# A windowed-attention and feed-forward kernel: separate PSUM tiles, another order at the start, and earlier loads in the loop

## The chip, the cores and the metric

The kernel runs on one core of a Trainium2 chip. The core has a matrix engine (TensorE, "PE"; its weight loads are shown apart as "PEld"), a vector engine (VectorE, "DVE"), a scalar engine (ScalarE, "ACT"), GpSimd ("POOL") and SyncE ("SP"), each with its own queue of instructions that it works through in order. Data comes from and goes to device memory by 16 DMA engines, which POOL and SP feed here. PE writes its products to PSUM, from which ACT and DVE copy or compute into SBUF. The metric is the device time of one launch in microseconds; lower is better.

## The reference

There are 4 batches, 8 heads, 768 positions and head size 64. A query may see the keys of the last 96 positions and the first 8 keys of its batch; a bias falls with the distance, with one slope for each head. The attention output, 3072 tokens of 512, goes through a feed-forward layer of width 2048.

```python
scores = scale * np.matmul(q, k.transpose(0, 1, 3, 2))
is_global = pos[None, :] < int(n_global)                  # n_global = 8
is_local = (rel >= 0) & (rel < int(n_local))              # n_local = 96
dist = np.where(is_global & ~is_local, float(n_local), np.abs(rel))
scores = scores - slopes[:, None, None] * dist            # 8 slopes
scores = np.where(is_global | is_local, scores, -1e9)
a = softmax(scores)                                       # written out in the reference
x = np.matmul(a, v)                                       # -> (3072, 512)
h = x @ w_in                                              # (512, 2048)
r = np.maximum(h, 0.0)
out = (s * (r * r) + b) @ w_out                           # (2048, 512)
```

Inputs and the output are float32; the kernel multiplies in bf16.

## The kernel before

The 3072 tokens are cut into 12 granules of 256, three to a batch; `j` is the granule's number. The order of the instructions is written out by hand: each engine works through its own in the order in which the functions below are called.

**The steps for a granule.** `load_pairs` or `load_rows` (lines 86 and 96) and `load_v` (107) bring k, q and v from device memory through POOL's DMA queue, which also turns float32 into bf16. A granule's v comes in two pieces. k and q must be transposed: for granules 0 to 2 PE does it into PSUM (`T_mm`, 251) and ACT or DVE copies the result out (`T_ev`, 266); from granule 3 on DMA transposes do it, issued on SP (`XB`, 280). `KO` and `VO` (303, 318) collect on DVE the keys and values of the neighbouring block and the global ones. `S_mm` (353) makes the scores of a pair of heads, `hp` 0 to 3, and `S_post` (373) takes the exponential on ACT. For granules 0 and 1 the bias and the mask are added on PE before that, by products with a diagonal matrix (`SB_mm`, 343); later DVE multiplies the exponentials by a template made once per head (`make_tmpl`, 242). The result is the tile `pt`. `A` (392) multiplies `pt` with v on PE, and DVE divides by the row's sum and writes `xn`. `xn` is transposed to `xT` by PE (`XT_half`, 442; `XT_pe`, 427) or by DMA (`XT_dma`, 460). `P1` (476) multiplies by two of the 16 column blocks of w_in, ACT takes the relu, and DVE squares (`flush`, 471). `P2` (522 and 562) multiplies by w_out, and DVE scales and adds the bias row (`P2_out`, 534).

**PSUM tiles.** Tags name them: `scA` and `scB` for scores (two banks each), `av` for value products, `psh` (two buffers), `pso`. One tile of tag psh holds the transposed k and the transposed q of a half of a granule; `T_mm` makes it for the first of the two and finds it in `tps` for the second. In `P2_end` (596), for the last 128 tokens, the two column pieces (0 to 320 and 320 to 512) lie in the two halves of one scB tile.

**The start.** SP issues four loads of the first granule's q and k (lines 148 and 149), in float32 and by halves (heads 0 to 3, and 4 to 7), as "raw" pieces; `cast` makes them bf16 on DVE or ACT. POOL builds the identity and the mask base, and issues in this order: v of granule 0 (two pieces), k and q of granule 1, piece 0 of w_in, v of granule 1, pieces 1 to 7 of w_in, k, q and v of granule 2, and three of four pieces of w_out (188 to 199). `more_loads` (201), called later, adds granule 3, the last piece of w_out, and granule 4. Lines 606 to 731 are the written order of the start. `idle` (224) puts products of constants on PE that nobody reads.

**The loop.** `period(j, items, at)` (746) runs for granules 3 to 11. It makes the scores of granule `j` and its value products, with feed-forward pieces of the granules before it (`items`) between them. After `A(j, 0)` it calls `pace(j)` and `load_granule(j + 2)`. `pace` (123) copies one element of `xn[j]` on POOL, so POOL issues the six loads of granule j + 2 only after that `xn` has been written.

Of the kernel before, what the change touches and what calls it, by code (L numbers as in the profile page):

```python
# [18 lines left out]
def kernel(  # L19
# [76 lines left out]
    def load_rows(j, nm):  # L96
        b, g = bg(j)
        src = q if nm == "q" else k
        t = ldp.tile([P, GB, H, D], BF16, name=f"{nm}nat", tag=f"{nm}nat")
        nat[nm, j] = t  # L100
        for i in range(GB):
            sb = g * GB + i
            nc.gpsimd.dma_start(  # L103
                t[:, i, :, :], src[b, :, sb * P : (sb + 1) * P, :].rearrange("h p d -> p h d")
            )

    def load_v(j):
        b, g = bg(j)
        for i in range(GB):
            sb = g * GB + i  # L110
            nc.gpsimd.dma_start(  # L111
                vaug[b][:, sb, :, 0:D],
                v[b, :, sb * P : (sb + 1) * P, :].rearrange("h p d -> p h d"),
            )
# [6 lines left out]
    pdum = const.tile([1, 1], BF16, name="pdum")  # L121

    def pace(j):
        nc.gpsimd.tensor_copy(pdum[:], xn[j][0:1, 0, 0, 0:1])  # L124

    def load_w_in(i, n):
        w = DF // n
        nc.gpsimd.dma_start(  # L128
            w_in_bf[:, :, i * w : (i + 1) * w], w_in_view[:, :, i * w : (i + 1) * w]
        )  # L130

    def load_w_out(i, n=4):
        w = FC // n
        nc.gpsimd.dma_start(
            w_out_bf[:, i * w : (i + 1) * w, :], w_out_view[:, i * w : (i + 1) * w, :]
        )
# [14 lines left out]
    def cast(nm, half, eng=None):  # L151
        hs = slice(4 * half, 4 * half + 4)
        i, o = raw32[:, "kq".index(nm), hs, :], nat[nm, 0][:, hs, :]
        if eng is None:
            nc.vector.tensor_copy(o, i)
        else:
            nc.scalar.copy(o, i)
# [27 lines left out]
        base=NL - 1,  # L185
        channel_multiplier=1,
    )
    load_v(0)
    load_pairs(1, "k")
    load_pairs(1, "q")  # L190
    load_w_in(0, 8)
    load_v(1)
    for i in range(1, 8):
        load_w_in(i, 8)
    load_pairs(2, "k")
    load_pairs(2, "q")
# [2 lines left out]
        load_w_out(i)  # L199

    def more_loads():
        load_rows(3, "k")
        load_w_out(3)
        load_rows(3, "q")
        load_v(3)
        load_granule(4)
# [17 lines left out]
    def idle(n, tag="pso", cols=4 * P):  # L224
        ps = PS[tag].tile([P, 4 * P], F32, name="ps_i", tag=tag)
        for _ in range(n):
            nc.tensor.matmul(
                ps[:, 0:cols],
                lhsT=nc.const_aps.tensor(1.0, (P, P), BF16),
                rhs=nc.const_aps.tensor(1.0, (P, cols), BF16),  # L230
                start=True,
                stop=True,
            )
# [8 lines left out]
    def make_tmpl(h):  # L242
        slope = float(2.0 ** (-8.0 * (h + 1) / H))
        nc.scalar.activation(
            tmpl[:, h, :], base[:].rearrange("p a c -> p (a c)"), ACT.Exp, scale=slope
        )
# [1 line left out]

    tps = {}

    def T_mm(j, half, nm, tag="psh"):
        a = 0 if nm == "k" else 1
        if (j, half) not in tps:
            tps[j, half] = PS[tag].tile([P, 2, 2, GT], BF16, name="ps_t", tag=tag)
        ps = tps[j, half]
        for e in range(2):
            hp = 2 * half + e
            for i in range(GB):
                for hi in range(2):
                    nc.tensor.transpose(  # L260
                        ps[hi * D : (hi + 1) * D, a, e, i * P : (i + 1) * P],
                        nat[nm, j][:, 2 * hp + hi, i * D : (i + 1) * D],
                        ident[:],
                    )

    def T_ev(j, half, nm, eng=None):
        b, g = bg(j)
        a = 0 if nm == "k" else 1
        if j not in qT:
            qT[j] = qtp.tile([P, HP, GT], BF16, name="qT", tag="qT")  # L270
        src = tps[j, half][:, a, :, :].rearrange("p e (i t) -> p e t i", i=GB)
        hs = slice(2 * half, 2 * half + 2)
        dst = kT[b][:, hs, g * GT : (g + 1) * GT] if nm == "k" else qT[j][:, hs, :]
        dst = dst.rearrange("p e (t i) -> p e t i", i=GB)
        if eng is None:
            nc.vector.tensor_copy(dst, src)
        else:
            nc.scalar.copy(dst, src)  # L278
# [64 lines left out]
    def SB_mm(j, hp, which=None):  # L343
        ps = sc_tile(j, hp, which)
        n = ncols(j)
        c0 = 0 if n == 3 * P else P
        m = base[:].rearrange("p a c -> p (a c)")[:, c0 : c0 + n]
        for hi in range(2):
            nc.tensor.matmul(  # L349
                ps[:, hi, 0:n], lhsT=diag[:, 2 * hp + hi, :], rhs=m, start=True, stop=False  # L350
            )
# [21 lines left out]
    def S_post(j, hp, biased=False):  # L373
        n = ncols(j)
        ps = sps.pop((j, hp))
        pt = ppool.tile([P, 2, 4 * P], BF16, name="pt", tag="pt")
        pts[j, hp] = pt
        nc.scalar.activation(pt[:, :, 0:n], ps[:, :, 0:n], ACT.Exp, scale=QSCALE)  # L378
        if not biased:
            c0 = 0 if n == 3 * P else P  # L380
            m = tmpl[:, 2 * hp : 2 * hp + 2, c0 : c0 + n]
            nc.vector.tensor_tensor(pt[:, :, 0:n], pt[:, :, 0:n], m, ALU.mult)  # L382
# [190 lines left out]
    def P2_cols(j, tb, ps, lo, hi):  # L573
        b, g = bg(j)
        flush()
        for fc in range(FC):
            nc.tensor.matmul(  # L577
                ps[:, 0 : hi - lo],
                lhsT=gT[j][:, fc, tb * P : (tb + 1) * P],
                rhs=w_out_bf[:, fc, lo:hi],  # L580
                start=(fc == 0),
                stop=(fc == FC - 1),
            )
        o_sb = work.tile([P, hi - lo], F32, name="o_sb", tag="o_sb", bufs=5)
        nc.vector.scalar_tensor_tensor(
            out=o_sb[:],
            in0=ps[:, 0 : hi - lo],
            scalar=s_bc[:],
            in1=bvec[:, lo:hi],
            op0=ALU.mult,  # L590
            op1=ALU.add,
        )
        t0 = b * S + g * GT + tb * P
        nc.sync.dma_start(out[t0 : t0 + P, lo:hi], o_sb[:])

    def P2_end(j, tb):
        ps = ps_b.tile([P, 2, DM], F32, name="ps_2e", tag="scB")
        P2_cols(j, tb, ps[:, 0, :], 0, 320)
        P2_cols(j, tb, ps[:, 1, :], 320, DM)

    def P2_sc(j, tb, which):
        pool, tag = ((ps_a, "scA"), (ps_b, "scB"))[which]
        po[j, tb] = pool.tile([P, 2, DM], F32, name="ps_2s", tag=tag)[:, 0, :]


    idle(7)
    SB_mm(0, 0)
    SB_mm(0, 1)
    cast("k", 0)
    T_mm(0, 0, "k")  # L610
    T_ev(0, 0, "k")
    cast("q", 0, "act")
    idle(2)
    T_mm(0, 0, "q")
    T_ev(0, 0, "q", "act")
    cast("k", 1)
    idle(1)
    T_mm(0, 1, "k")
    T_ev(0, 1, "k")
    cast("q", 1)  # L620
    idle(1)
    for hp in range(2):
        S_mm(0, hp, True)
        S_post(0, hp, True)
    T_mm(0, 1, "q")
    T_ev(0, 1, "q")
    more_loads()
    SB_mm(0, 2)
    S_mm(0, 2, True)
    S_post(0, 2, True)  # L630
    SB_mm(0, 3)
    S_mm(0, 3, True)
    S_post(0, 3, True)
    A(0, 0)
    A(0, 1, "pso")
    A(0, 2)
    A(0, 3, "pso")
    XT_half(0, 0, "act", "av")
    T_mm(1, 0, "k")
    T_mm(1, 1, "k")  # L640
    XT_half(0, 1, "dve", "pso")
    T_ev(1, 1, "k", "act")
    T_ev(1, 0, "k")
    SB_mm(1, 0)
    SB_mm(1, 1)
    T_mm(1, 0, "q")
    T_ev(1, 0, "q", "act")
    T_mm(1, 1, "q")
    T_ev(1, 1, "q", "act")
    KO(1)  # L650
    S_mm(1, 0, True)
    S_post(1, 0, True)
    S_mm(1, 1, True)
    S_post(1, 1, True)
    P1(0, 0)
    SB_mm(1, 2)
    S_mm(1, 2, True)
    S_post(1, 2, True)
    VO(1)
    A(1, 0)  # L660
    SB_mm(1, 3)
    S_mm(1, 3, True)
    S_post(1, 3, True)
    P1(0, 1)
    A(1, 1, "pso")
    make_tmpl(0)
    make_tmpl(1)
    A(1, 2)
    P1(0, 2)
    A(1, 3, "pso")  # L670
    P1(0, 3)
    XT_half(1, 0, "act", "av")
# [60 lines left out]
    def run(items, n):  # L733
        for _ in range(n):
            if items:
                f, *a = items.pop(0)
                f(*a)
# [7 lines left out]

    def period(j, items, at, late=None):
        SS(j, (0, 1))
        run(items, at[0])
        A(j, 0)
        if j + 2 < NJ:  # L750
            pace(j)
            load_granule(j + 2)
        run(items, at[1])
        A(j, 1)
        SS(j, (2, 3))
        if j + 1 < NJ:
            KO(j + 1)
        run(items, at[2])
        A(j, 2)
        run(items, at[3])  # L760
        A(j, 3)
        if late is None:
            XT_dma(j)
        if j + 1 < NJ:
            VO(j + 1)
        if j + 2 < NJ:
            XB(j + 2)
        if late is not None:
            run(items, 1)
            late()  # L770
            XT_pe(j, "act", "psh")
        run(items, 100)
# [80 lines left out]
```

## Time and profile before

| | |
|---|---|
| Median of 14 runs | 224.15 us (221.87 to 227.75) |
| The profiled execution | 227.26 us, of which its span is 225.5 us |
| PE busy | 211.3 us, 94% of the span |
| PEld busy | 143.4 us |
| DVE busy | 137.2 us |
| ACT busy | 115.4 us |
| POOL busy | 68.7 us |
| Mean rate of the DMA engines | 122 GB/s |
| Software queue (POOL's loads) | 13.11 MB in 72896 packets |
| Hardware queue (SP's transfers) | 14.17 MB in 34288 packets |

The span runs from the first instruction of the profiled execution to its last; its time, 227.26 us, has 1.76 us more around it. The profile's times are microseconds from the start of the span. Among its views are: busy tenths of each engine in 40 slices; groups of instructions by line with the mean duration; the chain of waits, which goes back from the last instruction to whatever released each step; windows, which give for any stretch the busy time of each engine, the TensorE clock that was granted (1.00 is full speed), the share of DMA time and the rate; and DMA issues with the time from issue to landing. A group's name reads out<-in, by the program's tile names. "Idle before" with an arrow names what an engine waited for.

### The profile page before, as it was taken

What the parts mean: (1) busy time and instruction counts of PE and PEld (TensorE: products, weight loads), DVE (VectorE), ACT (ScalarE), POOL (GpSimd) and SP (SyncE); (2) the same over time, 40 slices, a digit from 0 to 9 for tenths busy, and PEclk for the clock granted to TensorE, in tenths of its full rate; (3) what the DMA queues carried; (4) which work ended last, traced back from release to release, by engine and by line L of the source; (5) the groups of instructions that cost most, each with busy time, mean ns of one, the idle gap of its engine ahead of it and who ended that gap; (6) DMA issues with size and microseconds to landing.
All of it is one profiled execution on the core that took longest, in us unless ns stands there. A gap on an engine that the chain in (4) does not pass through costs nothing.

```text
span 225.5 us, 4962 instructions
## 1 busy us (share of the span) xinstructions
PE 211.3 (94%) x1997; PEld 143.4 (64%) x2029; DVE 137.2 (61%) x321; ACT 115.4 (51%) x176; POOL 68.7 (30%) x92
## 2 busy tenths in 40 slices
PE   8858999999999999999996999999999999999992
PEld 3435887645765775676763676675776676765762
DVE  3535557679988686656763484674684675752431
ACT  6525988842765645644443454645545645541420
POOL 8646664440072540620810360450530000000000
PEclk9967999999999999999998899999999999999998
DMA  5999999999969997997998299499796422031101
GB/s 156 101 177 195 189 189 195 179 148 120 86 42 150 209 156 125 145 175 95 158 171 113 62 117 165 102 153 128 113 168 114 71 77 66 0 95 47 47 27 69
DMA packets 107207, 27.60 MB, mean 122 GB/s; under 512 B 95792, under 2 KB 104240, under 8 KB 107184
## 3 DMA queue, kind: packets, MB, share of 16 engines
q0 software_dynamic: 72896, 13.11, 74.4%
q1 hardware_dynamic: 34288, 14.17, 33.3%
q8 instruction: 16, 0.26, 0.5%
q14 instruction: 7, 0.06, 0.1%
HBM read 27.26 MB, written 6.29 MB: 149 GB/s over the span
## 4 chain that ended last, share of the span: by engine, by line
PE 82%; DMA 7%; DVE 3%; issue 2%; ACT 2%; POOL 1%; SPq 1%; POOLq 0%; DVEq 0%; ACTq 0%
PE ps L483 36%; PE ps L526 29%; PE ps_av L410 5%; PE ps_s L365 5%; DMA vaug<-in_v_dram 4%; PE ps_2s L526 3%; DMA xT<-xn 3%; PE ps_2e L577 2%; DVE xn L419 1%; PE ps_t L260 1%; ACT pt L378 1%; PE ps_s L349 1%; PE ps_x L449 1%; SPq L463 1%; ACT gT L492 0%
## 5 line engine op out<-in xcount | busy, mean ns | idle before, releaser
L483 PE MATMUL ps<-xT,w_in_bf 128*128 128x256 bf16 x768 | 95.4, 274 | 2.3 <-DMA xT<-xn 2.2
L492 ACT ACTIVATE gT<-ps 128x512 bf16<-128x512 f32 x96 | 57.3, 599 | 62.2 <-PE ps L483 61.3
L483 PEld LDWEIGHTS <-w_in_bf 128*128 128x128 bf16 x768 | 73.6, 98 | 20.7 <-issue 3.1
L526 PE MATMUL ps<-w_out_bf,gT 128*128 128x512 bf16 x308 | 79.4, 382 | 1.9 <-issue 0.8
L474 DVE TENSOR_TENSOR gT<-gT 128x512 bf16<-128x512 bf16 x96 | 40.2, 424 | 24.9 <-ACT gT L492 24.7
L526 PEld LDWEIGHTS <-gT 128*128 128x128 bf16 x368 | 33.8, 98 | 30.7 <-issue 0.6
L378 ACT ACTIVATE pt<-ps_s 128x1024 bf16<-128x1024 f32 (+1 forms) x48 | 43.1, 952 | 18.8 <-PE ps_s L365 18.8
L382 DVE TENSOR_TENSOR pt<-pt,tmpl 128x1024 bf16<-128x1024 bf16 (+1 forms) x40 | 26.1, 652 | 13.0 <-ACT pt L378 11.9
L124 POOL COPY pdum<-xn 1x1 bf16<-1x1 bf16 x7 | 1.7, 249 | 76.4 <-DVE xn L419 76.4
L111 POOL DMA_DIRECT2D vaug<-in_v_dram x24 | 21.6, 915 | 3.9 <-DMA w_out_bf<-in_moe_w_out_dram 3.0
L410 PEld LDWEIGHTS <-pt 128*128 128x128 bf16 x352 | 16.4, 99 | 9.4 <-DVE xn L419 3.0
L418 DVE RECIPROCAL rc<-ps_av 128x4 f32<-128x4 f32 x48 | 8.6, 180 | 21.5 <-PE ps_av L410 20.8
L419 DVE TENSOR_TENSOR xn<-ps_av,rc 128x256 bf16<-128x256 f32 x48 | 20.4, 424 | 2.1
L537 DVE SCALAR_TENSOR_TENSOR o_sb<-ps,s_bc,bvec 128x512 f32<-128x512 f32 x18 | 13.5, 748 | 12.6 <-PE ps L526 12.6
L410 PE MATMUL ps_av<-vaug,pt 128*128 128x65 bf16 x224 | 18.1, 198 | 3.1 <-DMA vaug<-in_v_dram 2.0
L103 POOL DMA_DIRECT2D knat<-in_k_dram x18 | 15.8, 883 | 5.6 <-PE ps L483 3.3
L103 POOL DMA_DIRECT2D qnat<-in_q_dram x18 | 15.9, 899 | 2.1 <-DMA w_out_bf<-in_moe_w_out_dram 1.7
L365 PE MATMUL ps_s<-qT,kT 64*128 64x128 bf16 x224 | 12.5, 218 | 1.0 <-ACT qT L278 0.5
L410 PE MATMUL ps_av<-vo,pt 128*128 128x65 bf16 x128 | 12.0, 193 | 0.0
L365 PEld LDWEIGHTS <-kT 64*128 64x128 bf16 x224 | 7.1, 94 | 6.9 <-issue 5.9
L365 PE MATMUL ps_s<-qT,ko 64*128 64x128 bf16 x128 | 8.0, 216 | 0.0
L128 POOL DMA_DIRECT2D w_in_bf<-in_moe_w_in_dram x8 | 6.0, 752 | 5.6 <-DMA vaug<-in_v_dram 3.4
(66 smaller groups left out, 112.5 us busy)
## 6 DMA issues: line engine op xcount, KB each, us to landing
out_dram<-o_sb SPq DMA_DIRECT2D x23, 256.0 KB, 2.6
vaug<-in_v_dram POOLq DMA_DIRECT2D x24, 128.0 KB, 6.2
knat<-in_k_dram POOLq DMA_DIRECT2D x18, 128.0 KB, 4.6
qnat<-in_q_dram POOLq DMA_DIRECT2D x18, 128.0 KB, 4.7
w_in_bf<-in_moe_w_in_dram POOLq DMA_DIRECT2D x8, 256.0 KB, 9.6
w_out_bf<-in_moe_w_out_dram POOLq DMA_DIRECT2D x4, 512.0 KB, 12.7
raw<-in_k_dram SPq DMA_DIRECT2D x2, 256.0 KB, 4.1
raw<-in_q_dram SPq DMA_DIRECT2D x2, 256.0 KB, 4.3
```

Source lines behind the costliest of these rows:

```text
L103: nc.gpsimd.dma_start(t[:, i, :, :], src[b, :, sb * P : (sb + 1) * P, :].rearrange("h p d -> p h d"))
L111: nc.gpsimd.dma_start(vaug[b][:, sb, :, 0:D], v[b, :, sb * P : (sb + 1) * P, :].rearrange("h p d -> p h d"),)
L365: nc.tensor.matmul(ps[:, hi, oc * P : (oc + 1) * P], lhsT=kt[r, :], rhs=qT[j][r, hp, i * P : (i + 1) * P], start=not biased, stop=not bias ...
L378: nc.scalar.activation(pt[:, :, 0:n], ps[:, :, 0:n], ACT.Exp, scale=QSCALE)
L382: nc.vector.tensor_tensor(pt[:, :, 0:n], pt[:, :, 0:n], m, ALU.mult)
L410: nc.tensor.matmul(av[:, i, hi, :], lhsT=pt[:, hi, c * P : (c + 1) * P], rhs=vv, start=n_ == 0, stop=n_ == len(ops) - 1,)
L419: nc.vector.tensor_tensor(xn[j][:, :, 2 * hp : 2 * hp + 2, :], av[:, :, :, 0:D], rc[:].to_broadcast((P, GB, 2, D)), ALU.mult,)
L474: nc.vector.tensor_tensor(gs, gs, gs, ALU.mult)
L483: nc.tensor.matmul(ps[:, i, :], lhsT=w_in_bf[:, kc, fc * P : (fc + 1) * P], rhs=xT[j][:, kc, :], start=(kc == 0), stop=(kc == KC - 1),)
L492: nc.scalar.activation(gs, ps[:], ACT.Relu)
L526: nc.tensor.matmul(po[j, tb], lhsT=gT[j][:, fc, tb * P : (tb + 1) * P], rhs=w_out_bf[:, fc, :], start=(fc == 0), stop=(fc == FC - 1),)
L537: nc.vector.scalar_tensor_tensor(out=o_sb[:], in0=po[j, tb], scalar=s_bc[:], in1=bvec[:], op0=ALU.mult, op1=ALU.add,)
```

## The change

The function `T_mm` gets a flag `own`, with which it makes a tile of its own instead of sharing that of the other operand, and `T_ev` can copy out one of its two head pairs alone. The start uses these for the first granule's q: its first half goes to a tile of tag pso, its second to one of tag av, and the last copy is made in two parts. In the order of the start, the first k transposes come ahead of the first two `SB_mm`; `A(0,0)` comes ahead of the fourth pair's scores; the transposes of granule 1's k come between value products; its q transposes and their copies are interleaved with `XT_half`; `P1(0,0)` comes before granule 1's first scores, and `P1(0,1)` and `P1(0,2)` one step sooner; the filler products are two fewer and use tag av.

On POOL a one-element copy of the first raw k piece is put ahead of `load_v(0)`, so the loads wait for that piece. Piece 1 of w_in goes ahead of granule 1's v, and the last piece of w_out ahead of granule 3's k. In the loop, `pace` reads `pts[j, 0]` (the first pair's masked exponentials) instead of `xn[j]`, and it and `load_granule` are called right after the first two pairs' scores. `P2_end` takes an scA tile for the first column piece and an scB tile for the second.

```diff
     def pace(j):
-        nc.gpsimd.tensor_copy(pdum[:], xn[j][0:1, 0, 0, 0:1])
+        nc.gpsimd.tensor_copy(pdum[:], pts[j, 0][0:1, 0, 0:1])
...
+    nc.gpsimd.tensor_copy(pdum[:], raw32[0:1, 0, 0, 0:1])
     load_v(0)
     load_pairs(1, "k")
     load_pairs(1, "q")
     load_w_in(0, 8)
+    load_w_in(1, 8)
     load_v(1)
-    for i in range(1, 8):
+    for i in range(2, 8):
         load_w_in(i, 8)
...
     def more_loads():
+        load_w_out(3)
         load_rows(3, "k")
-        load_w_out(3)
         load_rows(3, "q")
...
-    def T_mm(j, half, nm, tag="psh"):
+    def T_mm(j, half, nm, tag="psh", own=False):
         a = 0 if nm == "k" else 1
-        if (j, half) not in tps:
+        if own or (j, half) not in tps:
             tps[j, half] = PS[tag].tile([P, 2, 2, GT], BF16, name="ps_t", tag=tag)
         ps = tps[j, half]
+        tps[j, half, nm] = ps
...
-    def T_ev(j, half, nm, eng=None):
+    def T_ev(j, half, nm, eng=None, es=(0, 1)):
...
-        src = tps[j, half][:, a, :, :].rearrange("p e (i t) -> p e t i", i=GB)
-        hs = slice(2 * half, 2 * half + 2)
+        e0, e1 = es[0], es[-1] + 1
+        src = tps[j, half, nm][:, a, e0:e1, :].rearrange("p e (i t) -> p e t i", i=GB)
+        hs = slice(2 * half + e0, 2 * half + e1)
...
     def P2_end(j, tb):
-        ps = ps_b.tile([P, 2, DM], F32, name="ps_2e", tag="scB")
-        P2_cols(j, tb, ps[:, 0, :], 0, 320)
-        P2_cols(j, tb, ps[:, 1, :], 320, DM)
+        for pool, tag, lo, hi in ((ps_a, "scA", 0, 320), (ps_b, "scB", 320, DM)):
+            ps = pool.tile([P, 2, DM], F32, name="ps_2e", tag=tag)
+            P2_cols(j, tb, ps[:, 0, :], lo, hi)
...
-    idle(7)
-    SB_mm(0, 0)
-    SB_mm(0, 1)
+    idle(7, "av")
     cast("k", 0)
     T_mm(0, 0, "k")
     T_ev(0, 0, "k")
+    SB_mm(0, 0)
+    SB_mm(0, 1)
     cast("q", 0, "act")
-    idle(2)
-    T_mm(0, 0, "q")
+    T_mm(0, 0, "q", "pso", True)
     T_ev(0, 0, "q", "act")
     cast("k", 1)
-    idle(1)
+    idle(1, "av")
     T_mm(0, 1, "k")
     T_ev(0, 1, "k")
     cast("q", 1)
-    idle(1)
     for hp in range(2):
         S_mm(0, hp, True)
         S_post(0, hp, True)
-    T_mm(0, 1, "q")
-    T_ev(0, 1, "q")
+    idle(1, "av")
+    T_mm(0, 1, "q", "av", True)
+    T_ev(0, 1, "q", None, (0,))
+    T_ev(0, 1, "q", None, (1,))
     more_loads()
     SB_mm(0, 2)
     S_mm(0, 2, True)
     S_post(0, 2, True)
+    A(0, 0, "pso")
     SB_mm(0, 3)
     S_mm(0, 3, True)
     S_post(0, 3, True)
-    A(0, 0)
-    A(0, 1, "pso")
-    A(0, 2)
-    A(0, 3, "pso")
-    XT_half(0, 0, "act", "av")
+    A(0, 1)
+    A(0, 2, "pso")
     T_mm(1, 0, "k")
     T_mm(1, 1, "k")
-    XT_half(0, 1, "dve", "pso")
+    T_ev(1, 0, "k", "act")
+    A(0, 3)
+    XT_half(0, 0, "act", "pso")
+    SB_mm(1, 0)
+    T_mm(1, 0, "q")
+    XT_half(0, 1, "dve", "av")
     T_ev(1, 1, "k", "act")
-    T_ev(1, 0, "k")
-    SB_mm(1, 0)
+    T_ev(1, 0, "q")
     SB_mm(1, 1)
-    T_mm(1, 0, "q")
-    T_ev(1, 0, "q", "act")
     T_mm(1, 1, "q")
     T_ev(1, 1, "q", "act")
     KO(1)
+    P1(0, 0)
     S_mm(1, 0, True)
     S_post(1, 0, True)
     S_mm(1, 1, True)
     S_post(1, 1, True)
-    P1(0, 0)
+    P1(0, 1)
...
     VO(1)
-    A(1, 0)
     SB_mm(1, 3)
     S_mm(1, 3, True)
     S_post(1, 3, True)
-    P1(0, 1)
+    A(1, 0)
     A(1, 1, "pso")
+    P1(0, 2)
     make_tmpl(0)
     make_tmpl(1)
     A(1, 2)
-    P1(0, 2)
...
     def period(j, items, at, late=None):
         SS(j, (0, 1))
-        run(items, at[0])
-        A(j, 0)
         if j + 2 < NJ:
             pace(j)
             load_granule(j + 2)
+        run(items, at[0])
+        A(j, 0)
```

## The prediction

> **What bounds the kernel now.** I read the slices first: where PE is full, and at which clock.
>
> ```profile
> PE   8858999999999999999996999999999999999992
> PEclk9967999999999999999998899999999999999998
> ```
>
> A slice is 5.64 us. From the sixth on PE is nearly always busy, so time is to be had only in the first four slices, around slice 22, and at the very end. The groups agree: PE is busy 211.3 of 225.5 us, and the next engine, DVE, 137.2. I then read the chain of waits over the start, and the windows over the stretch it points to.
>
> ```profile
> 2.55 0.95 POOL vaug L111
> 3.50 9.89 DMA vaug<-in_v_dram
> ...
> 13.43 0.39 PE ps_av L410 x4
> ```
>
> Start, length, what: the chain stands on the second piece of v for 9.89 us. Nothing after it can be attention until 13.43.
>
> ```profile
> 9.35:12.77 3.42, 1.66 (x20) 0.84 (x19) 0.69 (x1) 2.10 (x3) 0.07 (x1) 0.99 1.74 153
> 12.77:16.18 3.41, 2.09 (x28) 1.57 (x25) 2.07 (x8) 0.00 (x0) 2.23 (x3) 0.50 1.91 177
> 16.18:19.60 3.42, 3.20 (x26) 1.71 (x25) 1.62 (x4) 1.17 (x2) 2.22 (x4) 0.51 1.57 194
> ```
>
> Stretch, its length, then busy us of PE, PEld, DVE, ACT, POOL; granted clock, DMA share, GB/s. PE was half busy in the first stretch, and the clock fell to 0.50 near 12.7. It stayed there through a stretch that was 61% busy, and came back near 19.5, after one that was 94% busy. So the wait for v costs twice: idle PE, then slow PE.
>
> The same windows by the microsecond show what v waited for:
>
> ```profile
> 5.00:6.00 1.00, 1.00 (x11) 0.53 (x10) 0.19 (x1) 0.28 (x1) 1.00 (x2) 1.00 0.96 209
> ...
> 8.00:9.00 1.00, 0.57 (x15) 0.37 (x16) 0.91 (x2) 0.59 (x1) 1.00 (x2) 1.00 0.26 14
> 9.00:10.00 1.00, 0.81 (x10) 0.42 (x11) 0.58 (x1) 0.92 (x2) 0.42 (x1) 1.00 1.48 96
> ```
>
> Up to about 7 the DMA engines carry mainly the raw q and k pieces from SP's queue. By queue, GpSimd's moved 115 packets from 5 to 6, 281, 409, 111, and then some 700 in each us from 9 on. v's two pieces were issued at 2.49 and 3.44.
>
> **The profiled run against the median.** Its span is 225.5, its time 227.26 (1.76 outside the span), the median 224.15. Here the 3.1 us lie:
>
> ```profile
> 119.20:139.40 20.20, 17.86 (x160) 11.78 (x164) 10.75 (x26) 8.63 (x12) 5.54 (x7) 0.92 1.08 117
> 139.40:155.60 16.20, 16.04 (x160) 11.26 (x164) 9.55 (x22) 8.53 (x12) 5.50 (x7) 1.00 1.14 132
> ```
>
> One period of the loop took 20.2 us where the next took 16.2: the chain shows xT<-xn issued at 114.9 and landing only at 121.9, and the clock at 0.50 behind it. Without these 4.0 us the run is at 223.3, so I take the median run as one mostly without this stall, and take all gains from 224.15.
>
> **Part by part.**
>
> *The end.* Of the last token block, the second column piece waits until DVE has read the first, in the other half of the same PSUM tile:
>
> ```profile
> 217.85 2.19 PE ps_2e L577 x16
> ...
> 220.06 0.56 DVE o_sb L585
> ...
> 220.66 1.49 PE ps_2e L577 x16
> ```
>
> With two tiles the second piece starts at 220.04, not 220.66: **0.6 us**, with nothing beside it; ps_a's tile was read last by DVE at 209.30 + 0.75, so no new wait. Late next is PE itself.
>
> *k and q in separate PSUM tiles, transposes ahead of the mask products.* T_mm(0,0,"q") no longer waits for the k copy (0.19 us), k's transposes no longer stand behind four mask products (knat ready 4.64, PE there at 5.13), and the last q copy (0.69) is cut in two so that S_mm(0,2) starts after half. Together some 1 us, but all of it before v lands: **nothing**, hidden by v's wait. Two fewer filler products (0.22 to 0.4 each) are hidden by the same wait. If v came before about 10 they would count.
>
> *The copy ahead of load_v(0).* POOL now waits for the first raw k piece (DVE's cast of it started at 3.81), copies one element, and issues v. In the loop such a copy starts 0.54 us before the next load's issue, so v is issued near 4.4 instead of 2.49: **1.9 us later**, and behind it all of POOL's queue: k and q of granule 1, w_in, v of granule 1. What this does to v's landing the trace does not show; both ends:
>  - Late end: v keeps its 10.0 us from issue to landing. The second piece lands at 15.3.
>  - Early end: v is as quick as a v load in the loop (5.8 us, two at a time). Its second piece, issued near 5.3, lands at 11.1.
>  - Between: the raw pieces, alone, are through near 6.3 (0.93 MB were moved by 6, at up to 324 GB/s); GpSimd's queue starts 2.5 us after the issue, as before, near 7; v's 2048 packets (2 x 128 KB in rows of 64 bf16) at 700 per us take 2.9; landings then lagged the bytes by about 3 (0.262 MB were through near 10.1, the second piece landed at 13.4). This gives **12.9**, and I take it: it is worked from the queue's own packets.
>
>  A rule speaks against this edit. The Trainium skill, "DMA: Bandwidth & Descriptors", section "Issuing engines are not separate DMA queues", says that transfers run on the same 16 engines and interleave whichever engine issued them, so holding v back creates no bandwidth. Pure interleaving would make it late by up to 1.9. The rows show the engines not filled while v waits (14 GB/s from 8 to 9), which that rule does not explain; so I stay at 0.5 sooner.
>
> *Value products between the scores.* A(0,0) now stands in PE's queue before SB_mm(0,3) and S_mm(0,3). While v is out, these 8 matmuls wait behind it, and ACT's fourth exp with them: PE idles longer before v (about 9.9 to 12.9), so I expect the clock to fall again. After v the work fills the gaps in which A waited for DVE. I sum PE's queue from v to the end of P1(0,0), S_mm(1,0) and S_mm(1,1), in the cold durations of the trace: four A at 0.5; SB_mm(0,3) 2 x 0.32 (as the cold 384-column ones at 3.7) and S_mm(0,3) about 0.5 (estimate from 0.34 warm); 16 k transposes 1.0; XT halves 0.61 + 0.54; SB_mm(1,0) and (1,1) 4 x 0.43; 16 q transposes 1.0. Sum 8.0 cold, to which the warm P1(0,0), 0.98, and 16 score products, 0.62, are added. Before, all this ended at 22.30.
>
>  When does the clock return? In the trace, after a stretch 94% busy. The new queue is dense from 12.9, so one stretch earlier: near 16.2, with 3.2 of the 8.0 done and 4.8 left, which at full clock is about 2.5 (16 q transposes fell from 1.0 to 0.47). I add 0.3 for copies that ACT and DVE owe: 19.0; with 1.6 more 20.6: a gain of **1.7**. If it returns only at 19.5: 6.6 done, 1.4 left is 0.7, so 20.2 + 1.6 = 21.8: a gain of 0.5. Here too a rule stands against it: the Trainium skill, "TensorE: Matmul & The Clock Gate", Part 4, says that transposes don't count as busy for the clock. By it the dense stretch, with some 0.8 us of transposes, is only 70% busy, and the answer is 0.5. The row: the stretch from 16.18 had only 1.4 us of other products, yet it brought the clock back. I take 1.7.
>
> *P1(0,0) sooner* is in that sum: it fills the 0.46 us in which PE waited for ACT's qT copy at 20.24. w_in 0 landed at 17.6 and w_in 1 (now ahead of v(1)) near 20.6, in time. v(1) comes one w_in later, 1.4 us, from 19.4 to 20.8; VO(1) needs it at 19.85, before A(1,0) at 23.06: DVE may stand 1 us, with slack behind.
>
> *Loads in the loop.* pace(j) waits for the first masked pt instead of A(j,0)'s xn. In the period from 103.3 pt was ready at 105.2, xn's copy started at 107.60: six loads (5.3 us of issue) start 2.4 us sooner. Late next: nothing on PE, since k and q are transposed at the period's end. Their tail leaves xT<-xn freer, and collides with the q transposes of the period before, which have over 8 us of slack. In a normal period this is **0**; it may spare a stall like the one at 120 (0 to 4.0; for the median run 0). load_w_out(3) before load_rows(3,"k"): needed at 49.3, landed 45.1; k of granule 3 slips 2.7 us with 14 of slack: 0.
>
> *Does the gain last?* Tightest landings behind the start: w_out 1 (26.26 + 12.1 = 38.4, used at 42.0), w_in 4 (24.6, used at 28.0): 3.4 of slack. A gain of 1.7 passes.
>
> **Sum:** 224.15 - 1.7 - 0.6 = **221.8**. On the profiled run's own time: 227.26 - 2.3 = 225.0, or 221.0 without its stall.
>
> **Rivals.**
>  1. *Only the end is gained.* v at 13.4, clock back at 19.5: 6.1 done, 1.9 left is 1.0; 20.5 + 1.6 = 22.1, gain 0.2. With the end: 223.4. For it: no row shows how dense a stretch must be between 61% and 94%; against: the denser queue.
>  2. *Slower: the held v.* v at 15.3 with SB_mm(0,3) behind it. If the clock is back at 19.6: 4.3 done, 3.7 left is 1.9, + 0.3 + 1.6 = 23.4, 1.1 lost, 224.7 with the end; one stretch later, 23.3 + 1.6 = 24.9: 226.1. Middle 225.4. It decides from a v landing after about 14.2. For it: v's 10 us may be start-up of the queue; against: the contention from 5 to 7.
>  3. *v at 11.1 and no fall of the clock.* All loads come some 2 us sooner, PE runs warm; the start gains up to 5, held to about 4.5 by the later loads: 219.0. The short wait speaks for it, the 49% busy stretch against it.
>
> **Numbers.** Chances: forecast 0.50 (own range 220.6 to 223.0), rival 1 0.20, rival 2 0.17, rival 3 0.13. A measurement tells 0.5% (1.1 us) from no change: faster is under 223.0, slower over 225.3. Faster: nearly all of the forecast, rival 3, a third of rival 1: 0.67; slower: over half of rival 2 and a stall more: 0.13; same 0.20. Range 219.4 to 225.2.
>
> **What would show it.** DMA vaug in the chain: ending near 12.9 (11 rival 3, 15 rival 2). Granted clock 1.00 from about 16.2. P1(0,0) ending before S_mm(1,0) starts, near 20. Two L577 groups with no DVE between. pdum starting some 2 us after a period's first S_mm. I am wrong if v lands after 14, or if the clock stays at 0.50 to 19.5.

## The result, and the profile after

The changed kernel takes **218.88 us** (median of 10 runs, 217.82 to 220.8), against 224.15 before (48 runs by now, 220.11 to 227.75). The ratio is **0.9849, 95% interval 0.9808 to 0.9890**, that is 3.4 us less (2.5 to 4.3); the two medians differ by 5.3, a ratio of 0.9765. The comparison leaves out runs of the kernel before that lie over 1.5% above its fastest, here over 223.4, and with them many of those that the change repairs, so a ratio can stand closer to 1 than that of the medians. I take the gain of a typical run to lie between 3.4 and 5.3.

In the profiled execution the span is 217.6 (before 225.5, of which 4.0 were the stall at 120). The slices of the changed kernel, in tenths, each 5.44 us:

```profile
PE   7689999999799999999999999999999999999993
PEclk9999999999999999999999999999999999999999
```

The dent in the clock in slices 3 and 4 is gone, and so is the one in the middle. A new dip of PE stands in slice 11. The chain of waits over the start (start, length, what):

```profile
3.80 0.44 POOL pdum L188
4.24 1.82 POOL vaug L111 x2
6.06 5.57 DMA knat<-in_k_dram
11.63 0.04 issue
11.67 0.64 PE ps_t L263 x16
...
15.33 1.05 PE ps L487 x8
```

v's transfer is no longer in it. v was issued at 4.2 instead of 2.5, yet its second piece landed near 9.8 instead of 13.4, and the first value product started at 10.10. From the DMA issues (count, KB of one, median us from issue to landing), before and after:

```profile
vaug<-in_v_dram POOLq DMA_DIRECT2D x2, 128.0 KB, 10.0
```
```profile
vaug<-in_v_dram POOLq DMA_DIRECT2D x2, 128.0 KB, 4.7
```

The load that ends last is now that of k of granule 1. Below are the windows of the same three stretches as before: stretch, length, busy us of PE, PEld, DVE, ACT, POOL, granted clock, DMA share, GB/s.

```profile
9.35:12.77 3.42, 3.25 (x59) 2.07 (x58) 2.61 (x9) 2.36 (x4) 3.42 (x5) 1.00 1.63 165
12.77:16.18 3.41, 2.93 (x35) 1.74 (x34) 2.18 (x6) 1.66 (x3) 2.14 (x4) 1.00 1.77 184
16.18:19.60 3.42, 3.21 (x45) 1.93 (x44) 1.66 (x3) 3.20 (x5) 2.46 (x4) 1.00 1.64 189
```

PE is busy for 3.25 where it was for 1.66, and the clock never leaves 1.00. P1(0,0) and the first two score products of granule 1 are done by 16.9; before it was 22.30.

I use one mark to see how much of the lead is kept: the first score product of each granule. For granule 2 it starts at 33.91, 4.55 sooner than before; first the kernel before, then the changed one:

```profile
38.46 0.29 PE L365 MATMUL ps_s<-qT,kT 64*128 64x128 bf16 x4
```
```profile
33.91 0.29 PE L369 MATMUL ps_s<-qT,kT 64*128 64x128 bf16 x4
```

For granule 3 it starts at 54.36 (58.91), still 4.55. Then PE waits. From the timeline of PE (start, length, instruction, and in brackets the idle time before it with its releaser), and from the chain over the same stretch:

```profile
54.36 0.23 PE L369 MATMUL ps_s<-qT,kT 64*128 64x128 bf16 x2
56.02 0.46 PE L369 MATMUL ps_s<-qT,kT 64*128 64x128 bf16 x10 [1.43 <-DMA qT<-qnat]
```
```profile
28.79 13.46 DMA knat<-in_k_dram
...
42.26 1.30 SPq L294
...
46.40 9.58 DMA qT<-qnat
55.98 0.04 issue
56.02 0.46 PE ps_s L369 x10
```

The second piece of granule 3's q reaches qT only 9.58 us after its transpose was issued. That costs 1.4 us, and the lead from there on is 3.2 (the period of granule 4 starts at 67.60, before at 70.82). The end, from the timeline:

```profile
210.62 3.66 PE L581 MATMUL ps_2e<-w_out_bf,gT 128*128 128x320 bf16 x32
```

Both pieces run as one block, with no DVE between: 0.6 us. PE's wait of 0.64 there stands in all five profiles with the old end (before, e2, e6, e11, e12) and in none of the nine with the new one. So 4.55 - 1.4 + 0.6 = 3.75, and with the 4.0 of the stall at 120, which this profile hasn't, 7.75 of the 7.9 us between the two spans are placed.

### The profile page after: what moved, and what is told of

It reads as the page before. It is cut to its first block, busy times and chain, and to the rows that moved or that the text cites. A ratio compares the mean times of both kernels' runs of the same rounds, so it can differ in the third digit from the quotient of the medians.

```text
span 217.6 us, 4952 instructions
## 1 busy us (share of the span) xinstructions
PE 206.4 (95%) x1995; PEld 140.9 (65%) x2027; DVE 136.0 (62%) x322; ACT 115.8 (53%) x176; POOL 68.9 (32%) x93
## 4 chain that ended last, share of the span: by engine, by line
PE 76%; DMA 15%; ACT 2%; SPq 2%; issue 2%; DVE 2%; POOL 1%
PE ps L487 33%; PE ps L530 28%; DMA knat<-in_k_dram 9%; PE ps_av L414 4%; PE ps_s L369 4%; DMA qT<-qnat 4%; PE ps_2e L581 2%; PE ps_2s L530 2%; DMA raw<-in_k_dram 1%; SPq L294 1%; ACT gT L496 1%; POOL vaug L111 1%; ACT pt L382 1%; PE ps_s L353 1%; SPq L302 1%
## 5 line engine op out<-in xcount | busy, mean ns | idle before, releaser
L530 PE MATMUL ps<-w_out_bf,gT 128*128 128x512 bf16 x308 | 78.6, 379 | 1.9 <-issue 0.8
L124 POOL COPY pdum<-pt 1x1 bf16<-1x1 bf16 x7 | 1.6, 236 | 69.3 <-DVE pt L386 69.3
L414 PE MATMUL ps_av<-vaug,pt 128*128 128x65 bf16 x224 | 17.5, 193 | 0.6 <-DVE rc L422 0.3
L530 PE MATMUL ps_2s<-w_out_bf,gT 128*128 128x512 bf16 x30 | 7.3, 379 | 0.1
```

The costliest lines, as they stand in the source:

```text
L414: nc.tensor.matmul(av[:, i, hi, :], lhsT=pt[:, hi, c * P : (c + 1) * P], rhs=vv, start=n_ == 0, stop=n_ == len(ops) - 1,)
L530: nc.tensor.matmul(po[j, tb], lhsT=gT[j][:, fc, tb * P : (tb + 1) * P], rhs=w_out_bf[:, fc, :], start=(fc == 0), stop=(fc == FC - 1),)
```

## The experiments

Two questions stood after the result. Why did v come so early: because POOL's loads were held back behind the raw k piece, or because of the new order? And which parts give the rest? All four kernels of the first group ran on one chip, where the kernel before had a median of 224.33.

**Without the held loads.** The changed kernel, less one line:

```diff
-    nc.gpsimd.tensor_copy(pdum[:], raw32[0:1, 0, 0, 0:1])
     load_v(0)
```

> The changed kernel without the one-element copy ahead of load_v(0). Theory (the held loads let the raw q and k pieces through first, and that is most of the gain at the start): v's second piece lands at 12.5 to 13.5 again as in the kernel before, A(0,0) stands in PE's queue until then, the clock falls, P1(0,0) and granule 1's first scores end at 20.5 to 22 instead of 16.9; ratio to the kernel before 0.990 to 1.000. Rival (the order at the start carries the gain, the copy only delays POOL): v's second piece lands before 10.5 and the ratio stays at 0.983 to 0.987.

Measured: 222.49 us, ratio 0.9894 (0.9837 to 0.9952). v took 9.8 us to land again, and the windows show the old picture, with the clock down:

```profile
9.35:12.77 3.42, 1.41 (x18) 0.85 (x19) 1.06 (x3) 1.66 (x3) 0.11 (x2) 1.00 1.68 148
12.77:16.18 3.41, 2.83 (x49) 2.08 (x49) 1.73 (x7) 1.40 (x2) 2.19 (x3) 0.83 1.67 187
16.18:19.60 3.42, 2.93 (x27) 1.54 (x26) 1.64 (x5) 1.31 (x3) 1.95 (x3) 0.67 1.80 183
```

Granule 2 starts at 38.31, only 0.15 before the old 38.46. The new order alone gains almost nothing at the start.

**Only the held loads.** The kernel before, plus that one line:

```diff
+    nc.gpsimd.tensor_copy(pdum[:], raw32[0:1, 0, 0, 0:1])
     load_v(0)
```

> The kernel before with that one copy ahead of load_v(0) and nothing else. Theory (held loads): v's second piece lands near 9.8 (10.0 to 9.5), the clock stays at 1.00, the first scores of granule 1 start at 16 to 17 and the first scores of granule 3 some 3 to 4.5 us sooner than before; ratio 0.981 to 0.988. Rival (order): v no sooner than 12, ratio 0.995 to 1.005.

Measured: 220.76 us, 0.9854 (0.9812 to 0.9895). v's two pieces landed 4.8 and 4.9 us after their issue, the clock stayed at 1.00, and granule 2 started at 34.59: 3.87 of the 4.55 come from this line. The other 0.7 is what the new order adds once v is early. Over all profiles with an early v, granule 2 starts at 34.46 to 34.77 with the old order (e2, e6, e12) and at 33.26 to 34.24 with the new one, save for e9's 34.76, to which the last section comes back.

**The old place of pace.** The changed kernel, with the loop's loads again behind `A(j, 0)` and `xn`:

```diff
-        if j + 2 < NJ:
-            pace(j)
-            load_granule(j + 2)
         run(items, at[0])
         A(j, 0)
+        if j + 2 < NJ:
+            pace(j)
+            load_granule(j + 2)
```

> The changed kernel with pace on xn and behind A(j,0) as before. Theory (in a period without a stall PE is full either way): same time as the changed kernel within 0.3%, ratio to the kernel before 0.983 to 0.989, xT<-xn landing up to 1 us later after its issue than in the changed kernel. Rival (the sooner loads spare waits for xT<-xn in most executions): ratio 0.990 or more, with a wait of PE for xT<-xn of over 0.5 us in some period.

Measured: 220.92 us, 0.9853 (0.9814 to 0.9892). PE waits once for xT<-xn in the loop, 0.48 us, and 0.39 for qT. The ratio is that of the changed kernel (0.9849), as the theory had it; by the medians it is 0.985 against 0.976, so this run alone does not tell what pace is worth.

**k of granule 3 first.** The changed kernel, with this swapped back:

```diff
-        load_w_out(3)
         load_rows(3, "k")
+        load_w_out(3)
         load_rows(3, "q")
```

> The changed kernel with granule 3's k ahead of the last piece of w_out, as before. Theory A (the 1.4 us wait of granule 3's first scores for qT<-qnat comes from that swap, through k's later transposes on SP): k lands some 2 us sooner, SP's first transpose starts near 40 instead of 42.3, the wait is 0 to 0.3, ratio 1.0 to 1.4 us (0.005 to 0.006) below that of the changed kernel, some 0.979. Theory B (the wait comes from PE being 4.5 us sooner while the loads up to granule 4 take the DMA engines just as long): SP's first transpose moves, but q's still lands near 55 and the wait stays over 0.8; ratio as the changed kernel's.

Measured: 218.76 us, 0.9754 (0.9710 to 0.9797). The wait for qT is gone. Why shows in SP's transposes; first the changed kernel, then this edit in a second execution on another chip (start, length of issue, queue, line, operation):

```profile
42.26 2.62 SPq L294 DMA_TRANSPOSE kT<-knat  x2
45.00 4.24 SPq L302 DMA_TRANSPOSE qT<-qnat  x2
```
```profile
39.34 2.64 SPq L294 DMA_TRANSPOSE kT<-knat  x2
43.64 3.46 SPq L302 DMA_TRANSPOSE qT<-qnat  x2
```

In the second execution PE has q in time:

```profile
54.12 0.51 PE L369 MATMUL ps_s<-qT,kT 64*128 64x128 bf16 x12
```

SP works in order: with w_out 3 in front, k lands later, and its transposes are issued 2.9 us later. SP is at them until 44.88, and q's two stand behind them: they are issued at 45.00 and 46.40, against 43.64 and 45.91 with this edit, and the second lands at 55.98 instead of 53.72. Of these 2.3 us only 0.5 is later issue; the rest is a longer way to landing (9.6 us against 7.8), and the cause of that was not tried.

**The changed kernel and that edit again.** Both ran on a second chip (kernel before: 223.69, 43 runs), to see whether the edit's gain can be measured.

> The changed kernel once more, beside e4b on the same chip. Ratio 0.983 to 0.987 to the kernel before; its wait of granule 3's first scores for qT<-qnat between 0.4 (as with the old pace) and 1.4 us.

> The changed kernel with granule 3's k ahead of the last piece of w_out, once more, on the same chip as the changed kernel. If that swap is worth the wait alone: 0.4 to 1.4 us below the changed kernel (0.002 to 0.006 of the ratio). If the earlier 0.9754 was more than that wait, the gap is 2 us again (0.010).

Measured: 219.19 and 218.38 us; ratios 0.9879 (0.9815 to 0.9942) and 0.9851 (0.9788 to 0.9915). The wait of 1.32 us is there in the first trace and absent in the second, so it is shown that the place of w_out 3 makes the wait; in time the edit brings 0.8, and the intervals overlap, so its size is not shown. By the medians the ratios are 0.980 and 0.976; e4's was 0.975 on the first chip.

**What holds v up.** With v held, POOL's queue moved 804 packets from 7 to 8 and 1119 from 8 to 9, where the kernel before moved 409 and 111. My first idea was the raw pieces in SP's queue. But behind them SP issues two more loads, of the scale `s` and the bias `b`, each spread to 128 rows of 4 bytes. The DMA issues of the kernel before (count, KB, us to landing) show how slow they were; in the changed kernel they took 4.4 and 4.3 us.

```profile
s_bc<-in_moe_s_dram SPq DMA_DIRECT2D x1, 0.5 KB, 7.0
b_bc<-in_moe_b_dram SPq DMA_DIRECT2D x1, 0.5 KB, 8.9
```

So I gave these two to POOL, where they come behind the loads of w_out 0 to 2, and changed nothing else in the kernel before (no held loads):

```diff
     s_bc = const.tile([P, 1], F32, name="s_bc")
-    nc.sync.dma_start(s_bc[:], moe_s.to_broadcast((P, 1)))
+    nc.gpsimd.dma_start(s_bc[:], moe_s.to_broadcast((P, 1)))
     b_bc = const.tile([P, 1], F32, name="b_bc")
-    nc.sync.dma_start(b_bc[:], moe_b.to_broadcast((P, 1)))
+    nc.gpsimd.dma_start(b_bc[:], moe_b.to_broadcast((P, 1)))
```

> The kernel before, with the two small loads of s and b (128 rows of 4 bytes each) taken from SP's queue and put on POOL's, behind the third piece of w_out; load_v(0) is not held. Theory T (these 256 packets of 4 bytes are what keeps POOL's queue slow from 5 to 9): POOL's queue reaches 700 packets in a us at about 7 instead of 9, v's second piece lands near 10.5 to 11.5 instead of 13.4, ratio 0.985 to 0.993. Theory R (the raw pieces themselves, whose packets share the 16 engines with v's): v's second piece lands within 0.7 of 13.4, ratio 0.997 to 1.003.

Measured: 220.34 us (22 runs, 219.68 to 222.12), 0.9918 (0.9889 to 0.9946); the medians differ by 3.35. v's second piece, issued at 3.50, landed at 9.5, sooner than the 10.5 to 11.5 expected. The software queue (POOL's loads) from 6 to 8, in the kernel before and then in this one (packets, MB, time as a share of 16 engines):

```profile
q0 software_dynamic: 690, 0.09, 67.8%
```
```profile
q0 software_dynamic: 1955, 0.27, 197.8%
```

And this kernel's windows:

```profile
6.00:7.00 1.00, 0.89 (x11) 0.45 (x9) 0.94 (x2) 0.00 (x0) 1.00 (x2) 1.00 2.02 202
7.00:8.00 1.00, 1.00 (x14) 0.46 (x15) 0.32 (x1) 0.58 (x1) 1.00 (x2) 1.00 2.28 158
8.00:9.00 1.00, 0.64 (x20) 0.47 (x18) 0.71 (x2) 0.72 (x2) 1.00 (x2) 1.00 1.78 166
```

From 8 to 9 it moves 166 GB/s where the kernel before moved 14. Moving two loads of 512 bytes each does what the held loads do: it is these two, and not mainly the 0.93 MB of raw pieces, that kept v waiting. That the held loads work in the same way, by letting the small loads through before POOL's queue starts, is argued: with them the small loads landed at 7.3 and 7.8 (before, 9.9 and 12.4), and further down the two remedies together gain no more than one.

**Doubled, and with long rows.** One edit puts two more such small loads into the kernel before. The other puts two SP loads of 128 rows of 512 bytes in the place of the small ones, in the kernel with those moved. Both read data that nobody uses:

```diff
     nc.sync.dma_start(b_bc[:], moe_b.to_broadcast((P, 1)))
+    s2_bc = const.tile([P, 1], F32, name="s2_bc")
+    nc.sync.dma_start(s2_bc[:], moe_s.to_broadcast((P, 1)))
+    b2_bc = const.tile([P, 1], F32, name="b2_bc")
+    nc.sync.dma_start(b2_bc[:], moe_b.to_broadcast((P, 1)))
```
```diff
     nc.gpsimd.dma_start(b_bc[:], moe_b.to_broadcast((P, 1)))
+    big = const.tile([P, 2, 2 * D], F32, name="big")
+    for i in range(2):
+        nc.sync.dma_start(
+            big[:, i, :], q[1, i, 0:GT, :].rearrange("(p i) d -> p (i d)", i=GB)
+        )
```

> The kernel before with two more small loads of s and b (128 rows of 4 bytes each, into tiles that nobody reads) right behind the two on SP's queue. Theory T (a cost for each such packet): v's second piece lands 2 to 4 us later than 13.4, at 15.5 to 17.5. Rival (v waits only as long as the raw pieces and any small packet are in flight, whatever their number): 13.0 to 14.2.

> e6 with two loads of 128 rows of 512 bytes (of q, into a tile that nobody reads) in the place of the two small ones on SP's queue: as many packets, 128 times the bytes. If the size of 4 bytes is what hurts: v's second piece lands 9.3 to 10.2 (0.13 MB more at some 200 GB/s is up to 0.7 us). If it is the number of packets behind the raw pieces in the hardware queue: after 12.

Measured, one run each: 225.47 and 220.89 us. With four small loads v's second piece landed at 14.9, 1.5 later than before, and PE stood before it:

```profile
14.92 0.71 PE L414 MATMUL ps_av<-vaug,pt 128*128 128x65 bf16 x10 [3.54 <-DMA vaug<-in_v_dram]
```

The size falls between the two theories' numbers, and v's first piece landed at 10.9, 1.7 sooner than before. That does not fit a fixed cost for each small packet. POOL's queue did stay slow for longer, with 352 to 452 packets in each us from 10 to 14, where before it moved 503 to 732. With the long rows v took 6.3 us and the clock stayed at 1.00: as many rows of 512 bytes do no such harm in that one run. Whether it is the 4 bytes, or that all 128 rows read the same address, was not tried.

**Both remedies, and one.** e8 is e4 (k of granule 3 first) with the small loads moved by the diff above, so it has both remedies. e9 is e8 without the held loads, by the diff of the first experiment. e10 is e9 with the old place of pace, by the diff of the third.

> e4b with the same two small loads moved as in e6. Under T it lands v up to 0.5 us sooner than e4b, and PE has nothing to gain but the wait for k of granule 1: ratio within 0.004 of e4b's. Under R: the same as e4b.

> The changed kernel with granule 3's k ahead of the last piece of w_out, with the small loads of s and b on POOL's queue, and without the copy ahead of load_v(0). Theory T (only the small loads made v late): v is issued at 2.5 and its second piece lands near 9.4, k of granule 1 near 11.0 instead of 11.7, no PE wait for it over 0.3, the clock at 1.00; first scores of granule 2 at 33.2 to 33.8, time 0 to 0.5 below e4b, ratio 0.982 to 0.986. Rival (holding the loads has a worth of its own): v's second piece lands after 10.5 and the ratio is 0.988 or more.

> e9 with pace on xn and behind A(j,0) as in the kernel before. If the sooner loads in the loop are worth nothing: the same time as e9 within 0.4 us, no wait for xT<-xn over 0.3. If they spare waits for xT<-xn: 0.5 to 1.3 us above e9, with such a wait in the trace.

Measured: e8 219.59 us (22 runs), 0.9868 (0.9837 to 0.9898), on the second chip; e9 218.60, 0.9768 (0.9732 to 0.9805), and e10 219.18, 0.9794 (0.9767 to 0.9822), on a third (before: 223.63). The second remedy adds nothing to the first, and either will do. e8's median even lies 1.2 above e4b's on the same chip, but the intervals overlap. e9's ratio came out below the expected 0.982 to 0.986, although its granule 2 started at 34.76 and not at 33.2 to 33.8. e10 against e9 is the purest trial of pace: 0.6 us, with overlapping intervals.

**Two readings over all runs.** The mean granted clock is listed for every run. On the second chip, 9 of 43 runs of the kernel before kept it at 0.998 or more, and took 220.6 to 222.9; the other 34, at 0.976 to 0.992, took 222.6 to 227.0. (On the first chip 1 of 11 kept it, on the third none of 11.) In the kernels with an early v the clock was 0.997 or more in 96 of 97 runs; the exception is a run of e8 at 0.989, with 220.35 us. Without the held loads (e1) it was so in 2 of 6, at 219.9 and 220.3 us; the rest took 222.1 to 223.7. A mean does not say where the clock was lost, but the place at the start fits: half a clock from 12.7 to 19.5, as in the profile before, would by my estimate make a mean of 0.985. The medians of the two groups are 221.15 and 224.08, a distance of 2.9; e6, with an early v and the old order, lies only 0.8 below the first. So the late v costs mainly by the clock, and by chance some runs escape.

And in the loop: seven profiles have the old pace (before, e2, e3, e6, e10, e11, e12), and in each PE waits for over 0.4 us around a P1 between 114 and 135; summed and averaged, 1.3. Of the seven with the new place (after, a2, e1, e4, e4b, e8, e9) five show none, a2 has 0.26, and e4 1.84, which is put down to ACT's pt: 0.3 on average. That speaks for about 1 us in favour of the new place, though one of the old place's waits too (e12) is put down to ACT's pt. The timed pair, with its 0.6, doesn't contradict it and doesn't prove it. On the first chip e3 and e4, which differ in pace and in the place of w_out 3, are 2.2 us apart with intervals that don't overlap; how that divides is open.

**The best version** is the changed kernel with k of granule 3 first: 218.76 and 218.38 us on two chips, below the changed kernel's 218.88 and 219.19, by less than the intervals can tell. e9, at 218.60, is equal to it.

## Why the prediction was right or wrong

The direction and the place (the start, and what v's wait does to the clock) were right. The median of 218.88 lies below the whole range (219.4 to 225.2) and close to rival 3's 219.0. The ratio, which puts the gain at 3.4 and so the time at 220.8, lies within the forecast's own range, but that is luck: rival 3's mechanism happened, to which I gave 0.13, and the forecast's did not. That rival 3's sum fits the median is partly luck too, since it knew neither of q's wait nor of what pace brings.

- *v's landing* is **the step that failed first**. I took 12.9 between the ends 11.1 and 15.3; 9.8 was measured, outside even the early end. The start of the queue near 7 was right. Two terms were too large: the 2.9 us for v's 2048 packets at 700 per us, and "landings then lagged the bytes by about 3". In the changed kernel the queue moved 106 packets from 6 to 7, 804 from 7 to 8 and 1119 from 8 to 9, so nearly 2048 were through by 9.0, after 2 us, and the landing lagged by about 0.8. The early end's row, a v load in the loop (5.8), was the nearer one, since that is the queue undisturbed. I had seen that 14 GB/s from 8 to 9 went unexplained, and I should have asked who else had a transfer open then: the small loads of `s` and `b`, issued from 2.9 on and slow to land, stand in the trace's list of DMA issues.
- *The rule on interleaving* (the Trainium skill, "DMA: Bandwidth & Descriptors", "Issuing engines are not separate DMA queues") would have made the held loads late by up to 1.9. The traces show the opposite, 3.6 us sooner; e6 shows that two transfers of one queue slowed the other far beyond their bytes. The measurement decides.
- *The start's gain*, 1.7, was mis-sized for that reason: P1(0,0) and the two score products ended at 16.9, not 20.6, and of that 4.55 was left at granule 2. My "I expect the clock to fall again" didn't come true, and the sum in cold durations had no object. What brings a fallen clock back, and so whether transposes count for it, no longer mattered and was not tried.
- *k and q in separate tiles at nothing, "hidden by v's wait"*: the condition I named, "if v came before about 10 they would count", was met. With the order they give 0.7 on an early v (33.91 against 34.59) and 0.15 on a late one.
- *P1(0,0) sooner*: as described, 15.33 before S_mm(1,0) at 16.30, but by the warm clock.
- *"k of granule 3 slips 2.7 us with 14 of slack: 0"* is **the second step that failed**: -1.4 us. I counted k alone. Its transposes slipped by 2.9; q's, behind them on SP, slipped by 1.4 and 0.5, and the second took 9.6 us to land beside granule 4's loads. In the kernel before, that second one was issued at 47.3 and landed near 56.4 for a use at 58.91: a slack of 2.5 for q where I had reckoned with k's 14. A lead of 4.55 was more than that. "Does the gain last? ... 3.4 of slack. A gain of 1.7 passes" looked at POOL's loads only and left the transposes out.
- *Pace, "0 for the median run"*: somewhat low. 0.6 by the timed pair, about 1 by the traces; not settled.
- *The end*, 0.6: as worked out.

Together 4.55 - 1.4 + 0.6, and up to 1 for pace, is 3.75 to 4.75, inside what the ratio and the medians leave open.

## What to carry to other kernels

When a queue stands still while the engines have room, list every transfer that is open at that moment, the smallest too: two loads of 512 bytes held up a quarter of a megabyte. A lead gained early lasts only as far as the tightest landing behind it, so follow each moved load through all that comes after it, the transposes on another engine's queue included. And where a wait drops the clock, look at the clock of every run, not of one profile: the runs of one kernel that spread over 3% may be of two kinds, those that kept the clock and those that lost it.

## What the hardware showed that I had not expected

- **Loads of 4-byte rows in SP's queue slow POOL's queue.** The two of them: 281 packets from 6 to 7 and 409 from 7 to 8 on POOL's queue; moved away, 844 and 1111.
- **Transposes by DMA took far longer beside a granule's loads.** In the changed kernel the four of granule 3 took 7.7 to 9.6 us to landing, while the loads of granule 4 were under way; the medians over all of k's and all of q's are 2.6 and 3.9. That the loads are the cause was not tried.
- **PE at half pace at a granted clock of 1.00.** e9 and e10 have the same instructions on PE at the start. From the timeline of PE, first e9, then e10:

```profile
4.70 0.64 PE L262 MATMUL ps_t<-ident,knat 128*64 128x128 bf16 x8 [0.77 <-DVE knat L155]
5.27 1.46 PE L352 MATMUL ps_s<-base,diag 128*128 128x384 bf16 x4
```
```profile
4.70 0.41 PE L262 MATMUL ps_t<-ident,knat 128*64 128x128 bf16 x8 [0.77 <-DVE knat L155]
5.04 0.82 PE L352 MATMUL ps_s<-base,diag 128*128 128x384 bf16 x4
```

 The windows give both a clock of 1.00 there. In e9 it lasts to about 9.4, and by then PE is 1.5 us behind (S_mm(0,2) at 10.67 against 9.18). So two profiles of the start can differ by more than a microsecond with the same instructions on PE; the cause was not looked for.
